# A fused attention, dense MoE and routed MoE kernel: first job's rows loaded earlier, later row loads on GpSimd, scatters declared independent, one low-part subtraction on VectorE

## The chip, the core and the metric

The kernel runs on one core of a Trainium2 chip. That core has five engines with an instruction stream each: PE (TensorE, matrix products), DVE (VectorE), ACT (ScalarE), POOL (GpSimd) and SP (SyncE, here only a queue that issues DMAs). A stream runs in its fixed order; an instruction that waits for another engine or for a transfer holds up all that stand behind it on its own engine. The metric is the time of one execution in microseconds (us); times given are medians of several runs.

## The reference

Three stages follow each other, in float32:

- attention on q, k, v of shape (4, 8, 768, 64), causal with a local window of 96 keys and 8 global keys, a linear bias by distance and a softmax; its output is 3072 tokens of 512 features;
- a dense expert layer: `h = x @ w_in` (512 to 2048), `g = h - tanh(h)`, `x = g @ w_out` (2048 to 512);
- a routed layer with 8 experts: `logits = x @ w_gate`, each token goes to `argmax`; per expert `relu(x @ w1[e]) @ w2[e]` (512 to 1024 to 512), scaled by the softmax value of the chosen expert and a sigmoid of `x @ w_output_gate`.

The result is the 3072 by 512 output of the routed layer.

## The kernel before

**Products in parts.** Each float32 operand of a big product is split into a high part (rounded, made on ACT) and a low part (the difference, made on DVE or POOL); a product is the three matmuls high x high, high x low, low x high. Names end in `h` and `l`: `gh` and `gl` of the gate, `xTh` and `xTl`, `h2h` and `h2l` of an expert's hidden layer, `eh` and `el` of an expert's weights.

**The block phase.** Tokens are worked through in 12 blocks (`NBLK`) of 256. For a block, 16 units of 128 hidden features follow each other: `moe_h` (L607, 12 matmuls into `ph`), the gate on ACT and DVE ending in `gg` (L637), its high part `gh` on ACT (L643) and its low part `gl` (L645, on DVE in the first block and on POOL in the others), then `moe_y` (L662, 6 matmuls into `y`). Attention of later blocks is interleaved.

**Routing of a block.** `rt_evac` copies `y` to `yrow` (ACT L677, DVE L679), `rt_T` transposes it (`yT`, L689), `rt_logits` makes the logits (`lp` L704, `lg` L712), DVE makes the choice, `rk` (L762, L763) counts on PE what place the token has within its expert, and DVE turns that into the row `su` (L787). Two indirect DMAs of POOL (`scatter`, L793) then write the block's 256 rows to those places of `srt`, a DRAM buffer with a region per expert. The framework makes each scatter wait for the one before it, since both write `srt`; only the last two are declared independent.

**The expert phase.** Work is cut into nine jobs. Job 0 is the first 256 rows of the fullest expert, job 1 the rest of that expert, jobs 2 to 8 are the other seven experts. After block 9 the fullest expert must have 256 rows (an assertion in the code says so), so job 0 needs no scatter later than that of block 9. A job is: `ex_rows` loads its rows from `srt` (`xr`, L923, issued by SP), `ex_T` transposes them on PE (`xTp`, L941) and splits them (ACT L954, DVE L955; L960 and L961 copy two columns), `ex_s1` is the first product (`h2p`, L973; `h2h` L977 on ACT, `h2l` L978 on DVE), `ex_s2` the second (`ob`, L1000), `ex_out` scales the result (L1013, L1015) and POOL stores it (L1018). `ex_load` brings an expert's weights in eight 512 KB pieces (`ex`, L881 and L884, issued by SP) into three shared row buffers (tag `row`); `ex_split` makes `eh` (ACT L899) and `el` (DVE L900) of each.

**What sets the order.** For the block phase and jobs 0 and 1 an agenda does: `at(time, rank, function)` puts a function on a slot, and slots are run in order (block `b` starts at 32 b, a unit takes two slots; rank -2 is run with raised priority). Later jobs are written out in a loop. The framework then settles each engine's order from this and from its own estimate of when things are ready, so that a function put earlier can move other engines' instructions too. At L866 `expert(r)` reads the number of the r-th fullest expert into a register of SP, which the DMA addresses need.

**Lines that the change touches.** L644 (who makes `gl`), L793 to L800 (the scatters), L864 to L870 (`expert`), L918 to L923 (`ex_rows`), L1192 to L1196 (job 0's buffers and its slot, `G + 26`, six slots before the end of block 11), L1215 (buffers of the row loads). What lies around them is printed here:

Of the kernel before, what the change touches and what calls it, by code (L numbers as in the profile page):

```python
# [32 lines left out]
def kernel(  # L33
# [15 lines left out]
    nc = tc.nc  # L49
    P = 128  # L50
# [3 lines left out]
    E, _, F = w1.shape  # L54
    TB = 256
    NBLK = NT // TB
# [8 lines left out]
    RS = NT + CAP  # L65
# [10 lines left out]
    persist = ctx.enter_context(tc.tile_pool(name="persist", bufs=1))  # L76
# [3 lines left out]
    srt = dram.tile([E * RS, W], F32, name="srt")  # L80
# [31 lines left out]
    order_i = persist.tile([P, E], I32, name="order_i")  # L112
# [19 lines left out]
    def at(gt, rank, fn):  # L132
        agenda.setdefault((gt, rank), []).append(fn)
# [465 lines left out]
    def moe_h(blk, u, gt):  # L599
        fg, fo = divmod(u, 4)  # L600
        ph = bank("h", 2, f"ph{blk}_{u}")
        n = 0
        for kc in range(KC):
            o = kc * 512 + fo * P
            whi, wlo = wih[fg][:, o : o + P], wil[fg][:, o : o + P]
            for lw, xx in ((whi, xhi), (whi, xlo), (wlo, xhi)):
                nc.tensor.matmul(ph[:, 0:TB], lw, xx[blk][:, kc, :], start=(n == 0), stop=(n == 3 * KC - 1))  # L607
                n += 1

        def tmp(tag, bufs, dt=F32):  # L610
            t = p1.tile([P, TB], dt, tag=tag, bufs=bufs, name=f"{tag}{blk}_{u}")
            return t

        L = {}

        def gate():
            hps = ph[:, 0:TB]
            uu = L["uu"] = tmp("uu", 2)
            ss = L["ss"] = tmp("ss", 2)
            tt = L["tt"] = tmp("tt", 2)  # L620
            vv = L["vv"] = tmp("vt", 2)
            nc.scalar.activation(uu, hps, AF.Square)  # L622
            nc.scalar.activation(tt, hps, AF.Tanh)  # L623
            nc.scalar.activation(ss, uu, AF.Square, scale=G_S, bias=ga[:, 0:1])  # L624
            nc.vector.scalar_tensor_tensor(out=vv, in0=uu, scalar=G_C, in1=hps, op0=ALU.add, op1=ALU.mult)  # L625
            nc.vector.tensor_tensor(out=tt, in0=tt, in1=hps, op=ALU.subtract)  # L626
            nc.vector.scalar_tensor_tensor(out=vv, in0=ss, scalar=G_S2B, in1=vv, op0=ALU.add, op1=ALU.mult)

        def gate2():
            uu, ss, tt, vv = L["uu"], L["ss"], L["tt"], L["vv"]  # L630
            gg = L["gg"] = tmp("gg", 2)
            if blk < 1:
                nc.scalar.activation(ss, uu, AF.Relu, bias=nt2[:, 0:1])
            else:
                nc.vector.tensor_scalar(out=ss, in0=uu, scalar1=G_T2, scalar2=None, op0=ALU.is_gt)
            nc.vector.tensor_tensor(out=gg, in0=vv, in1=uu, op=ALU.mult)
            nc.vector.copy_predicated(gg, ss.bitcast(I32), tt)  # L637

        def parts():
            gg = L["gg"]  # L640
            gh = tmp("gh", 3, F32R)
            gl = tmp("gl", 3, F32R)
            nc.scalar.copy(gh, gg)  # L643
            by = nc.vector if blk < 1 else nc.gpsimd  # L644
            by.tensor_tensor(out=gl, in0=gg, in1=gh.bitcast(F32), op=ALU.subtract)  # L645
            g_t[blk, u] = (gh, gl)

        at(gt + 1, 0, gate)
        at(gt + 2, 0, gate2)
        at(gt + 3, 0, parts)  # L650
# [16 lines left out]


    rts = {}
    last_rows = []  # L670

    def rt_evac(blk):
        for j in range(2):
# [24 lines left out]
    def rt_logits(blk, gt):  # L698
# [92 lines left out]
        def scatter(j):  # L791
            r = rts.pop((blk, "row", j))
            store = nc.gpsimd.indirect_dma_start(  # L793
                out=srt[:, :], out_offset=IndirectOffsetOnAxis(ap=L["su"][:, j : j + 1], axis=0),
                in_=r[:, 0:W], in_offset=None, bounds_check=E * RS - 1, oob_is_err=False,
            )
            if blk == NBLK - 1:
                last_rows.append(store.ins)
                if j == 1:
                    tc.declare_no_dep(last_rows[1], last_rows[0], reason="each token has one row")  # L800

        last = blk == NBLK - 1
        rk = -2 if last else 0
# [31 lines left out]
    ordering = {}  # L835
# [25 lines left out]
        nc.vector.tensor_scalar(out=kk, in0=kk, scalar1=-1.0, scalar2=float(E), op0=ALU.mult, op1=ALU.add)  # L861
        nc.vector.tensor_copy(order_i, kk)

    def expert(r):  # L864

        if r not in ordering:  # L866
            ordering[r] = nc.values_load(
                order_i[0:1, r : r + 1], engines=[mybir.EngineType.SP], min_val=0, max_val=E - 1
            )
        return ordering[r]  # L870


    w1h, w1l, w2h, w2l = {}, {}, {}, {}
# [43 lines left out]

    def ex_rows(n):  # L918
        r, j0, _ = jobs[n]
        rv = expert(r)  # L920
        for j, m in tiles(n):
            t = job_tile(n, "xr", [P, W], F32, f"xr{n}_{j}")
            nc.sync.dma_start(t[0:m, :], srt[ds(rv * RS + (j0 + j) * P, m), :])  # L923
            xrows[n, j] = t

    def tiles(n):
# [248 lines left out]
    for blk in range(NBLK):  # L1175
        G = 32 * blk
# [11 lines left out]
    for i in range(NP):  # L1188
# [2 lines left out]

    pools.update({  # L1192
        ("xTh", 0): (p1, "xhi", 2), ("xTl", 0): (p1, "xlo", 2), ("hh", 0): (p1, "gh", 3), ("hl", 0): (p1, "gl", 3),
        ("orow", 0): (persist, "row", 3),
    })
    at(G + 26, 0, lambda: ex_rows(0))  # L1196
    for g in range(n_groups(0)):
        at(G + 28 + g, 4, lambda g=g: ex_T(0, g))
    G += 32
# [12 lines left out]

    pa.release()
    p2a = ctx.enter_context(tc.tile_pool(name="p2a", bufs=1, side="right", reuse_waits="tile"))
    for k in range(3):  # L1215
        pools["xr", k] = p2a, "xr", 4
    for nm in ("xTh", "xTl"):
        pools[nm, 1] = p2a, "xTa", 4
# [200 lines left out]
```

## Time and profile before

| | |
|---|---|
| median of three runs | 1173.21 us (1171.07 to 1173.40) |
| profiled execution | 1168.82 us |
| its span, first to last instruction | 1167.1 us |
| mean granted TensorE clock | 0.988 |
| PE busy | 1106.7 us (95% of the span) |
| DVE busy | 856.2 us (73%) |
| ACT busy | 671.6 us (58%) |
| POOL busy | 214.2 us (18%) |
| all DMA | 103.25 MB, mean 88 GB/s |

The busy time of an engine is when it executes; PE's 60 us without work are in the first 120 us, around the change from the blocks to the experts (about 800 to 820 us), at a few job changes, and at the end. The profiled execution lies 4.4 us under the median of the runs, and its span 1.7 us under its own time. A granted clock of 1.00 is TensorE at 2.4 GHz and 0.50 is 1.2 GHz; a mean lies between these two levels.

### The profile page before, as it was taken

The page shows a single profiled execution, that of the slowest core. Times are in us where ns is not written, and L with a number is a line of the kernel's source. Part 1 is how long each engine was busy: PE and PEld are TensorE (multiplying, and loading weights), DVE is VectorE, ACT ScalarE, POOL GpSimd, SP SyncE. Part 2 cuts the span into 40 slices and gives each one's busy share as a digit, 9 for nine tenths or more (in the row PEclk, how much of TensorE's full clock was granted, in tenths as well). Part 3 has the DMA queues.
Part 4 walks back from the last instruction along what each step waited for, and adds up shares of the span by engine and source line. Part 5 has one row for each costly group of instructions (what it writes and reads, how often), then busy time and mean ns, then how long its engine had stood idle before and what let it go on. Part 6 is the DMA issues. An engine that isn't in the chain of part 4 may idle for free. (4 is left out here: it accounts for less than half of the span.)

```text
span 1167.1 us, 22211 instructions
## 1 busy us (share of the span) xinstructions
PE 1106.7 (95%) x7374; PEld 943.5 (81%) x7374; DVE 856.2 (73%) x2704; ACT 671.6 (58%) x1794; POOL 214.2 (18%) x281
## 2 busy tenths in 40 slices
PE   2888999999999999999999999998999999999995
PEld 1457888888888888888888888886888787888894
DVE  6899778899989889989889898998554434424411
ACT  4999876666666656666666666565352423423411
POOL 1000013222222222222222232324100100101100
PEclk9889999999999999999999999999999999999998
DMA  6954921111211112121112120113372614526200
GB/s 170 291 165 142 254 58 42 30 51 30 55 38 40 37 39 52 31 55 27 51 24 56 37 53 22 33 67 127 113 246 103 206 53 153 181 61 222 79 23 25
DMA packets 128850, 103.25 MB, mean 88 GB/s; under 512 B 101679, under 2 KB 101679, under 8 KB 128720
## 3 DMA queue, kind: packets, MB, share of 16 engines
q1 hardware_dynamic: 124592, 89.06, 26.7%
q0 software_dynamic: 4128, 12.61, 2.8%
q8 instruction: 62, 1.02, 0.4%
q14 instruction: 68, 0.56, 0.2%
HBM read 90.04 MB, written 21.88 MB: 96 GB/s over the span
## 5 line engine op out<-in xcount | busy, mean ns | idle before, releaser
L645 POOL TENSOR_TENSOR gl<-gg,gh 128x256 fp32r<-128x256 f32 x176 | 149.1, 847 | 485.7 <-ACT gh L643 368.1
L607 PE MATMUL ph<-xhi,wh 128*128 128x256 f32 x768 | 219.9, 289 | 3.5 <-DVE tt L626 3.5
L607 PE MATMUL ph<-xhi,wl 128*128 128x256 f32 x768 | 218.2, 285 | 0.0
L607 PE MATMUL ph<-xlo,wh 128*128 128x256 f32 x768 | 216.2, 282 | 0.0
L662 PE MATMUL y<-wh,gh 128*128 128x512 f32 x384 | 158.2, 412 | 1.0 <-ACT gh L643 0.9
L607 PEld LDWEIGHTS ph<-xhi,wh 128*128 128x128 f32 x768 | 144.8, 189 | 15.9 <-DVE tt L626 5.9
L662 PE MATMUL y<-wl,gh 128*128 128x512 f32 x384 | 154.1, 401 | 0.0
L607 PEld LDWEIGHTS ph<-xlo,wh 128*128 128x128 f32 x768 | 145.0, 189 | 6.7
L607 PEld LDWEIGHTS ph<-xhi,wl 128*128 128x128 f32 x768 | 144.8, 189 | 4.3 <-issue 2.6
L662 PE MATMUL y<-wh,gl 128*128 128x512 f32 x384 | 141.8, 411 | 2.5 <-POOL gl L645 2.3
L643 ACT CAST gh<-gg 128x256 fp32r<-128x256 f32 x192 | 78.2, 407 | 84.9 <-DVE gg L637 66.4
L622 ACT ACTIVATE uu<-ph 128x256 f32<-128x256 f32 x192 | 73.8, 384 | 78.3 <-PE ph L607 70.8
L978 DVE SCALAR_TENSOR_TENSOR h2l<-h2p,h2h 128x448 fp32r<-128x448 f32 (+3 forms) x72 | 40.0, 557 | 103.9 <-ACT h2h L977 103.8
L522 ACT ACTIVATE pr<-pr,sst 128x256 f32<-128x256 f32 (+1 forms) x192 | 93.0, 487 | 38.2 <-DVE sst L514 38.2
L625 DVE SCALAR_TENSOR_TENSOR vt<-uu,ph 128x256 f32<-128x256 f32 x192 | 79.8, 416 | 43.9 <-ACT tt L623 42.6
L900 DVE TENSOR_TENSOR el<-ex,eh 128x1024 fp32r<-128x1024 f32 x64 | 77.7, 1223 | 46.1 <-ACT eh L899 42.2
L977 ACT ACTIVATE h2h<-h2p 128x448 fp32r<-128x448 f32 (+3 forms) x72 | 35.3, 492 | 124.8 <-PE h2p L973 123.9
L899 ACT CAST eh<-ex 128x1024 fp32r<-128x1024 f32 x64 | 66.5, 1050 | 60.2 <-DMA ex<-in_moe_w_dram 45.0
L624 ACT ACTIVATE ss<-uu,ga 128x256 f32<-128x256 f32 x192 | 99.3, 517 | 0.0
L973 PE MATMUL h2p<-xTh,eh 128*128 128x448 f32 (+3 forms) x288 | 97.7, 342 | 0.0
L973 PE MATMUL h2p<-xTl,eh 128*128 128x448 f32 (+3 forms) x288 | 97.2, 338 | 0.0
L973 PE MATMUL h2p<-xTh,el 128*128 128x448 f32 (+3 forms) x288 | 97.1, 338 | 0.0
(199 smaller groups left out, 2505.6 us busy)
## 6 DMA issues: line engine op xcount, KB each, us to landing
ex<-in_moe_w_dram SPq DMA_DIRECT2D x64, 512.0 KB
vv<-vg SPq DMA_DIRECT2D x92, 96.0 KB
srt<-zrow SPq DMA_DIRECT2D x32, 257.0 KB
m<-in_moe_w_in_dram SPq DMA_DIRECT2D x16, 512.0 KB
m<-in_moe_w_out_dram SPq DMA_DIRECT2D x16, 512.0 KB
xr<-srt SPq DMA_DIRECT2D x25, 257.0 KB
qk<-in_q_dram SPq DMA_DIRECT2D x92, 64.0 KB
qk<-in_k_dram SPq DMA_DIRECT2D x92, 64.0 KB
```

Source lines behind the costliest of these rows:

```text
L522: nc.scalar.activation(pr[j][:, c0:], pr[j][:, c0:], AF.Exp, bias=st[:, j : j + 1], scale=-1.0, accum_out=st[:, 2 + j : 3 + j],)
L607: nc.tensor.matmul(ph[:, 0:TB], lw, xx[blk][:, kc, :], start=(n == 0), stop=(n == 3 * KC - 1))
L622: nc.scalar.activation(uu, hps, AF.Square)
L624: nc.scalar.activation(ss, uu, AF.Square, scale=G_S, bias=ga[:, 0:1])
L625: nc.vector.scalar_tensor_tensor(out=vv, in0=uu, scalar=G_C, in1=hps, op0=ALU.add, op1=ALU.mult)
L643: nc.scalar.copy(gh, gg)
L645: by.tensor_tensor(out=gl, in0=gg, in1=gh.bitcast(F32), op=ALU.subtract)
L662: nc.tensor.matmul(yb[blk, j], gx[:, j * P : (j + 1) * P], wx[fg][:, sl], start=(u == 0 and n == 0), stop=(u == NF - 1 and n == 2),)
L899: nc.scalar.copy(hi, st)
L900: nc.vector.tensor_tensor(out=ld[e, t][:, sl], in0=st, in1=hi.bitcast(F32), op=ALU.subtract)
L973: nc.tensor.matmul(ph[:, 0:N], lw, xx, start=(i == 0), stop=(i == 3 * KC - 1))
L978: nc.vector.scalar_tensor_tensor(out=hl, in0=ph[:, 0:N], scalar=0.0, in1=hh.bitcast(F32), op0=ALU.max, op1=ALU.subtract)
```

## The change

Four edits: job 0's rows are loaded at slot `G + 15` rather than `G + 26` (ahead of the scatters of block 10), into other buffers; from job 2 on the rows are loaded by POOL's DMA queue instead of SP's, for which the expert's number is read into a register of POOL too; all scatters to `srt` are declared independent of each other; and `gl` of the last block is made by DVE instead of POOL.

```diff
-            by = nc.vector if blk < 1 else nc.gpsimd
+            by = nc.vector if blk in (0, NBLK - 1) else nc.gpsimd
             by.tensor_tensor(out=gl, in0=gg, in1=gh.bitcast(F32), op=ALU.subtract)
...
-            if blk == NBLK - 1:
-                last_rows.append(store.ins)
-                if j == 1:
-                    tc.declare_no_dep(last_rows[1], last_rows[0], reason="each token has one row")
+
+            tc.declare_no_dep(store.ins, group="srt", reason="each token has one row")
+            tc.add_to_no_dep_group("srt", store.ins)
...
-    def expert(r):
-
-        if r not in ordering:
-            ordering[r] = nc.values_load(
-                order_i[0:1, r : r + 1], engines=[mybir.EngineType.SP], min_val=0, max_val=E - 1
-            )
-        return ordering[r]
+    def expert(r, by=mybir.EngineType.SP):
+
+        if (r, by) not in ordering:
+            ordering[r, by] = nc.values_load(order_i[0:1, r : r + 1], engines=[by], min_val=0, max_val=E - 1)
+        return ordering[r, by]
...
-        rv = expert(r)
+        by, name = (nc.gpsimd, mybir.EngineType.Pool) if n >= 2 else (nc.sync, mybir.EngineType.SP)
+        rv = expert(r, name)
         for j, m in tiles(n):
             t = job_tile(n, "xr", [P, W], F32, f"xr{n}_{j}")
-            nc.sync.dma_start(t[0:m, :], srt[ds(rv * RS + (j0 + j) * P, m), :])
+            by.dma_start(t[0:m, :], srt[ds(rv * RS + (j0 + j) * P, m), :])
...
-        ("orow", 0): (persist, "row", 3),
+        ("orow", 0): (persist, "row", 3), ("xr", 0): (p1, "yt", 3),
     })
-    at(G + 26, 0, lambda: ex_rows(0))
+
+    at(G + 15, 0, lambda: ex_rows(0))
...
-    for k in range(3):
+    for k in range(1, 3):
         pools["xr", k] = p2a, "xr", 4
```

What this does to the order of instructions is shown at three places.

The first is PE, at the end of the block phase, where `y` takes in the last two units of block 11 (`gh_14` to `gl_15`) and job 0 begins (`xTp` are its transposed rows, `h2p` its first product, `ob` its second). Before:

```order
L662 MATMUL y_0_12665<-wh_3_1328,gl_14_13294 128x512 [waits Pool_49]
L662 MATMUL y_1_12666<-wh_3_1328,gl_14_13294 128x512
L662 MATMUL y_0_12665<-wh_3_1328,gh_15_13317 128x512 [waits Activation_49]
...
L941 MATMUL xTp_0_13234<-ident,xr_0_13176 128x128 [waits DMAHW4_49,PE_49]
L941 MATMUL xTp_1_13263<-ident,xr_0_13176 128x128 [waits PE_49]
L662 MATMUL y_0_12665<-wh_3_1328,gl_15_13318 128x512 [waits Pool_49]
L662 MATMUL y_1_12666<-wh_3_1328,gl_15_13318 128x512
L941 MATMUL xTp_0_13234<-ident,xr_1_13178 128x128 [waits DMAHW5_49]
```

Of the changed kernel, the same place; the lines left out at the first dots are twelve matmuls each of `h2p_0` and `h2p_1` and the matmuls of `y` among them:

```order
L970 MATMUL h2p_0_13327<-xTh_0_13239,eh_0_12810 128x256 [waits DVE_49]
...
L970 MATMUL h2p_1_13350<-xTh_0_13239,eh_0_12810 128x256 [waits DVE_49]
...
L662 MATMUL y_0_12665<-wh_3_1328,gl_14_13294 128x512 [waits DVE_49]
L662 MATMUL y_1_12666<-wh_3_1328,gl_14_13294 128x512
L662 MATMUL y_0_12665<-wh_3_1328,gh_15_13317 128x512 [waits Activation_49]
...
L997 MATMUL ob_0_13395<-eh_4_13044,h2h_0_13340 128x512 [waits Activation_49]
...
L662 MATMUL y_0_12665<-wh_3_1328,gl_15_13318 128x512 [waits DVE_49]
L662 MATMUL y_1_12666<-wh_3_1328,gl_15_13318 128x512
L997 MATMUL ob_0_13395<-eh_4_13044,h2l_0_13341 128x512 [waits DVE_49]
```

All of job 0's eight transposes, 24 matmuls of `h2p` and two of `ob` now stand ahead of the last two of `y`; before, two transposes did.

The second is PE from the end of block 11's routing (`rk`, whose `ohb` is the choice of expert) to the first work of job 1 (`xTp` of `xr` after it). Before:

```order
L1000 MATMUL ob_0_13395<-eh_4_13040,h2h_3_13470 128x512 [waits Activation_49]
L763 LDWEIGHTS ones_bf
L763 MATMUL rk_13491<-ohb_13480,ones_bf 128x8 [waits DVE_49]
L1000 MATMUL ob_0_13395<-el_4_13041,h2h_3_13470 128x512
...
L1000 MATMUL ob_0_13395<-eh_6_13131,h2l_6_13588 128x512 [waits DVE_49]
L1000 MATMUL ob_1_13396<-eh_6_13131,h2l_6_13588 128x512
L941 MATMUL xTp_0_13673<-ident,xr_0_13669 128x128 [waits DMAHW2_49,PE_49]
L941 MATMUL xTp_1_13682<-ident,xr_0_13669 128x128
L941 MATMUL xTp_0_13673<-ident,xr_1_13671 128x128 [waits DMAHW3_49]
```

Of the changed kernel; the dots stand for five matmuls of `ob`, the two rows of `cnt_c` (the final counts), and five more of `ob`:

```order
L997 MATMUL ob_0_13395<-eh_6_13135,h2h_6_13587 128x512 [waits Activation_49]
L762 LDWEIGHTS ones_bf
L762 MATMUL rk_13491<-ohb_13480,ones_bf 128x8 [waits DVE_49]
L997 MATMUL ob_0_13395<-el_6_13136,h2h_6_13587 128x512
...
L997 MATMUL ob_1_13396<-eh_6_13135,h2l_7_13611 128x512
L938 MATMUL xTp_0_13673<-ident,xr_0_13669 128x128 [waits DMAHW2_49,PE_49]
L938 MATMUL xTp_1_13682<-ident,xr_0_13669 128x128 [waits DVE_49]
L938 MATMUL xTp_0_13673<-ident,xr_1_13671 128x128 [waits DMAHW3_49]
```

Before, 36 matmuls of `h2p`, 23 of `ob` and the counts stand between the last `rk` and the first `xTp` of job 1; now 11 of `ob` and the counts do, and the routing has moved back behind three more units of job 0.

The third is SP, where the rows of a later job and the weights of its successor are issued (`xr_0` to `xr_3`, `ex_1` to `ex_4`). Before:

```order
L881 DMA ex_2_14046<-in_moe_w_dram 128x1024 [waits DMAHW6_49,DMAHW3_49,DVE_49]
L923 ISA
L923 DMA xr_0_14062<-srt 128x514 [waits DMAHW7_49,PE_49]
L923 ISA
L923 DMA xr_1_14064<-srt 128x514 [waits DMAHW0_49,PE_49]
L923 ISA
L923 DMA xr_2_14066<-srt 128x514 [waits DMAHW1_49,PE_49]
L923 ISA
L923 DMA xr_3_14068<-srt 64x514 [waits PE_49]
L881 ISA
L881 DMA ex_3_14087<-in_moe_w_dram 128x1024 [waits DMAHW4_49,DVE_49]
```

Of the changed kernel:

```order
L877 DMA ex_1_14017<-in_moe_w_dram 128x1024 [waits DMAHW6_49,DVE_49]
L877 ISA
L877 DMA ex_2_14056<-in_moe_w_dram 128x1024 [waits DMAHW7_49,DMAHW2_49,DVE_49]
L877 ISA
L877 DMA ex_3_14107<-in_moe_w_dram 128x1024 [waits DMAHW3_49,DMAHW0_49,DVE_49]
L880 ISA
L880 DMA ex_4_14142<-in_moe_w_dram 128x2x512 [waits DMAHW1_49,DVE_49]
```

The four row loads, which wait for PE, no longer stand between `ex_2` and `ex_3`; they are in POOL's stream, between the stores of finished jobs.

## Rows read from the trace of the kernel before

**Rows 1.** First part of the page: busy time, share of span, instructions.

```profile
PE 1106.7 (95%) x7374; PEld 943.5 (81%) x7374; DVE 856.2 (73%) x2704; ACT 671.6 (58%) x1794; POOL 214.2 (18%) x281
```

**Rows 2.** Waits by releaser, PE and SP: total us, times, longest.

```profile
PE ob L1000 <- ACT h2h L977: 3.5, 2, 1.8
...
PE ob L1000 <- issue: 0.8, 2, 0.4
...
SPq L923 <- PE xTp L941: 114.7, 7, 26.6
```

**Rows 3.** Window at the transition: length, then busy us by engine, clock.

```profile
800.00:820.00 20.00, 15.15 (x87) 11.42 (x86) 15.55 (x33) 10.31 (x21) 9.32 (x9) 1.00 0.40 133
```

**Rows 4.** Timeline of PE, end of blocks: start, us, work, idle before.

```profile
809.41 0.73 PE L662 MATMUL y<-wh,gl 128*128 128x512 f32 x2 [1.67 <-POOL gl L645]
...
814.63 0.41 PE L941 MATMUL xTp<-ident,xr 128*128 128x128 f32 x2 [1.66 <-DMA xr<-srt]
814.79 0.71 PE L662 MATMUL y<-wh,gl 128*128 128x512 f32 x2
...
818.23 0.29 PE L973 MATMUL h2p<-xTh,eh 128*128 128x256 f32 x1
818.35 0.28 PE L973 MATMUL h2p<-xTl,eh 128*128 128x256 f32 x1
```

**Rows 5.** Timelines of PE, DVE, POOL and SP, routing to job 1.

```profile
830.88 0.18 PE L763 MATMUL rk<-ohb,ones_bf 128*128 128x8 bf16 x1
...
832.34 0.17 DVE L787 CAST su<-sf 128x2 uint32<-128x2 f32 x1
...
834.75 0.98 POOL L793 DMA_INDIRECT srt<-yrow,su  x1 [0.30 <-issue]
...
837.91 0.88 SPq L923 DMA_DIRECT2D xr<-srt  x2
...
841.32 0.88 PE L941 MATMUL xTp<-ident,xr 128*128 128x128 f32 x6 [0.16 <-DMA xr<-srt]
...
842.74 0.39 PE L1000 MATMUL ob<-el,h2h 128*128 128x512 f32 x1
842.97 0.63 PE L1000 MATMUL ob<-eh,h2l 128*128 128x512 f32 x2
843.44 0.40 PE L973 MATMUL h2p<-xTh,eh 128*128 128x256 f32 x2
```

**Rows 6.** Lines view: `gl` of the first and last block, `gg` of the last.

```profile
L645 DVE TENSOR_TENSOR gl<-gg,gh 128x256 fp32r<-128x256 f32 x16 | 6.7, 420 | 2.1 <-ACT gh L643 1.9
L645 POOL TENSOR_TENSOR gl<-gg,gh 128x256 fp32r<-128x256 f32 x16 | 16.5, 1033 | 27.1 <-ACT gh L643 26.1 <-POOL gl L645 0.9
L636 DVE TENSOR_TENSOR gg<-vt,uu 128x256 f32<-128x256 f32 x16 | 7.8, 485 | 0.0
```

**Rows 7.** Windows after three waits of PE, clock third from the end.

```profile
50.00:58.00 8.00, 7.40 (x23) 3.17 (x22) 6.42 (x14) 7.87 (x21) 0.00 (x0) 0.57 1.01 351
104.00:110.00 6.00, 4.34 (x22) 3.26 (x23) 4.50 (x15) 6.00 (x19) 0.61 (x3) 0.72 0.44 150
966.00:974.00 8.00, 8.00 (x39) 6.37 (x39) 7.07 (x13) 5.65 (x8) 0.00 (x0) 1.00 0.87 300
```

**Rows 8.** Timelines of PE: the waits ahead of the first two windows.

```profile
49.76 0.66 PE L546 MATMUL pt<-ident,pr 128*128 128x128 f32 x4 [2.23 <-ACT wl L270]
105.46 0.47 PE L546 MATMUL pt<-ident,pr 128*128 128x128 f32 x1 [2.45 <-ACT pr L533]
```

**Rows 9.** Timelines of SP, DVE and ACT at a job change.

```profile
955.97 2.09 SPq L923 DMA_DIRECT2D xr<-srt  x4
958.32 0.37 SPq L881 DMA_DIRECT2D ex<-in_moe_w_dram  x1
...
952.76 1.23 DVE L900 TENSOR_TENSOR el<-ex,eh 128x1024 fp32r<-128x1024 f32 x1 [1.11 <-ACT eh L899]
...
964.36 1.04 ACT L899 CAST eh<-ex 128x1024 fp32r<-128x1024 f32 x1 [3.21 <-DMA ex<-in_moe_w_dram]
```

More of the change, by code (lines that the diff above doesn't have):

```diff
@@ L669 @@
     rts = {}
-    last_rows = []
     def rt_evac(blk):
```

## The prediction, written before the result was known

> **What bounds the kernel now.** Read the share of the engines first: PE is busy 1106.7 us, 95% of the span [rows 1]. The other engines matter only where PE waits for them, so the next view is the list of waits, and then the timeline of PE at the places that the change touches. There are two kinds. The first is the end of block 11. In the 20 us from 800 on PE works 15.15 us [rows 3], so 4.85 us are lost. The timeline shows who ends the longest waits: 1.67 us for a low part from POOL and 1.66 us for job 0's rows, which SP had asked for only just before [rows 4]. Of the 4.85 us some 0.4 come behind the last two matmuls of `y`, which end at 815.5 (814.79 + 0.71, [rows 4]); 4.45 come ahead of them. DVE is full in that block too: no idle time stands ahead of its 16 products into `gg` [rows 6]. The second kind is in the expert phase: two waits of PE for `h2h`, 3.5 us together [rows 2]. All that the change can gain is these 8 us; the rest of PE's idle time is elsewhere.
>
> **The wait ahead of job 1: what the change moves here.** This is the term that decides. Job 1's rows can be loaded only when block 11 has been routed and scattered. The rows give the chain: the last `rk` matmul ends at 831.06, `su` is made at 832.34, the second scatter ends at 835.73 (834.75 + 0.98), SP issues the loads at 837.91 and the transposes of the second 128 rows start at 841.32 [rows 5]: 10.3 us from `rk` to there. Before, 36 matmuls of `h2p` at 0.12 us (818.23 to 818.35, [rows 4]) and 23 of `ob` at 0.23 us (842.74 to 842.97, [rows 5]) stand in this time, 9.7 us of work, and PE waits only 0.16 us. In the changed order the loads of job 0 come early, the framework puts 24 `h2p`, two `ob` and six more transposes ahead of the last `y`, and the routing slides back behind three more units of job 0. Between the last `rk` and job 1's transposes 11 matmuls of `ob` are left: 11 x 0.23 = 2.5 us, with the counts and two transposes about 2.8. PE then waits 10.3 - 2.8 = 7.5 us. Nothing else of job 1 or later can stand in, since PE's order is fixed.
>
> Now the sum from the end of `y` to job 1's first `h2p`. Before, 815.5 to 843.44 is 27.9 us, of which 0.4 idle. Moved ahead of `y`: 24 x 0.12 = 2.9, two `ob` 0.5, six transposes 0.7, in all 4.1. Left are 27.9 - 0.4 - 4.1 = 23.4 us of work. Add the wait of 7.5. Add 0.8, an estimate, because the split of job 1's transposed rows was covered by six matmuls of `ob` (six of 0.23 between the transposes and 843.44, [rows 5]) and is now bare. 31.7 us against 27.9: +3.8.
>
> The end of `y` itself: 4.1 us of work move into 4.45 us of idle time, so it may come 0.35 earlier, not more. What could push it later is the load of the weight piece `ex_7`, which waits for a scatter of block 10 and whose cast stands in ACT's order ahead of gate work; I give this up to 1.5. I take -0.1. The term is +3.7 us. Its bounds: the wait could be 2 us shorter or longer, about what passes between the end of the scatter and SP's issue (835.73 to 837.91, [rows 5]), and with the two ends of `y` that gives +1.5 to +7.
>
> **The clock.** After a wait of 2.23 us early in the kernel [rows 8] the granted clock is 0.57 over the next 8 us [rows 7]: PE at its 1.2 GHz level for most of them, 8 x 0.43 = 3.4 us lost. After one of 2.45 us [rows 8] it is 0.72 over 6 us, 1.7 us lost [rows 7]. Behind the wait of 1.8 us at a job change [rows 2] it stays at 1.00 [rows 7]. A wait of 7.5 us is longer than either that was followed by a fall, so I expect one. It costs between 0 and 3.4; I take 2.5, halfway between the two falls. The Trainium skill, "TensorE: Matmul & The Clock Gate", section "Why this matters for your kernels", asks that PE not idle for some microseconds between bursts of matmuls, since its clock then falls to half; by this rule a loss follows here. The two waits of [rows 8] agree with it.
>
> **The low parts on DVE.** 16 subtractions leave POOL and go to DVE. One takes 420 ns on DVE and 1033 ns on POOL in the mean of the last block [rows 6]. DVE being full, 16 x 0.42 = 6.7 us would come on top. But its own operations seem drawn out while POOL works: the product into `gg`, of the same shape as a low part, takes 485 ns in this block against those 420 [rows 6], and a unit has five operations of this shape on DVE; 16 x 5 x 0.065 = 5.2 us would come back if all were drawn out alike. I take what is added and what is given back as about equal, so nothing on `y`. If DVE gets little back, `y` ends later by up to the 1.5 of the bound above: PE ends 815.5 only after two waits of 1.66 us or more that were not DVE's [rows 4], and these are reserve.
>
> **Scatters independent.** The second scatter of a block no longer waits for the first to land. No wait of PE ends on this except through the low parts queued behind it on POOL in block 11, and these leave POOL anyway. Zero, from -0.2 to 0.2.
>
> **Register reads on POOL.** Seven new ones stand among block 10's low parts. No row shows one on POOL; between these subtractions POOL has idle time (27.1 us around 16 of them, [rows 6]). Zero, at most +1.
>
> **Row loads from job 2 on.** SP loses 25 loads and the waits in front of them, 114.7 us [rows 2]. What stands behind such a load on SP is the next weight piece. At one job change `el` has freed a row buffer at 953.99 (952.76 + 1.23), but SP first issues four row loads, 2.09 us from 955.97 on, and the piece only at 958.32; ACT then waits 3.21 us for it until 964.36 [rows 9], and PE waits for the `h2h` queued behind that cast. Without the loads the piece can go at 954.0, 4.3 us sooner, more than the 3.21. So both waits, 3.5 us, should go. Bounds: 0, if a transfer or a buffer takes the place of the queue, and -4.3 with the two waits of 0.4 that have no releaser [rows 2]. I take -3.5.
>
> For POOL the loads are new. They stand ahead of stores of finished rows, and job 2's stand behind job 0's two stores, so they are issued while PE waits for job 1's rows. A DMA that POOL prepares took it about 1 us (0.98 with 0.30 between, [rows 5]): two stores and four loads are 8 us from the end of job 0's last `ob`; job 2's transposes come 7.5 + 1 + 1.7 = 10.2 us after it, or later at the lower clock. The last rows, 3.4 us in landing (837.91 to 841.32, [rows 5]), may be 1 to 2 us late. I take 0, because the lower clock stretches the matmuls in front, and keep 0 to +2. The Trainium skill, "DMA: Bandwidth & Descriptors", section "Latency and other measured facts", gives a GpSimd DMA about 1 us to its first byte against 0.6; no run shown here has such a load from GpSimd. By that the sum would be 0.4 higher if it fell on PE's path.
>
> **Sum.** +3.7 + 2.5 + 0 - 3.5 = +2.7 us on the profiled execution's 1168.82 is 1171.5. This execution lies 4.4 us under the median of the timed runs, so the forecast in the terms of that median is 1175.9 us.
>
> **Rivals.** All are worked out against the median.
> - *Faster.* The wait ahead of job 1 is at its short end (+1.5), does not pull the clock down, and the expert phase gains all 4.3 us: 1173.2 + 1.5 - 4.3 = 1170.4. For it: both small waits stand at the same `ob` as the two large ones [rows 2]. Against it: the wait would have to keep the clock up at three times the length after which it fell twice. It decides from the point where wait and clock together cost under 2 us.
> - *No change.* The wait is there and the clock does not fall: 3.7 - 3.5 = +0.2, 1173.4. For it: at the transition PE has worked without a break for 20 us or more before the wait, and in the first 120 us it had not.
> - *Slower by more.* SP's queue was not what held up the weights, or POOL's stores now do: the change does not do what it says in the expert phase, and the two waits stay. 3.7 + 2.5 + 0 = +6.2: 1179.4. For it: from its issue at 958.32 to the cast at 964.36 the piece needed 6 us, more than the queue had cost it [rows 9]. Against it: the row buffer was free 4.3 us before the issue.
>
> **How the numbers follow.** What a measurement of this kernel can tell from no change is about 0.2%, 2.3 us: faster is below 1170.9, slower above 1175.5. The forecast has 0.50, between 1174 and 1178.5; of this 0.33 lies above 1175.5 and 0.17 below. Faster has 0.21, no change 0.18 (0.01 of it below 1170.9), slower by more 0.11. Sums: faster 0.22, same 0.34, slower 0.44. The range from 1169.5 to 1179.5 takes in the forecast, no change, about half of the faster case and half of the slowest. The forecast alone has 1174 to 1178.5.
>
> **What would show it.** Right: PE waits 5 to 9 us for `xr` ahead of job 1's transposes, and no more than 0.5 us at a time ahead of the last `y`; the granted clock is near 0.5 for some microseconds behind that wait; there is no wait of PE for `h2h` over 1 us at later job changes, and ACT's waits for `ex` are shorter. Wrong: a wait ahead of job 1 under 4 us; a granted clock of 1.00 all through; waits for `h2h` still there; waits of PE for `xr` in jobs 2 to 8; or DVE so late in block 11 that `y` ends over 1.5 us later, counted from the start of the block.

## The result, and the profile after

The changed kernel takes 1183.01 us (median of four runs, 1181.03 to 1184.86), the kernel before 1172.14 us beside it (1170.42 to 1173.40). The ratio is 1.0093 with a 95% interval of 1.0071 to 1.0116: about 11 us slower. The forecast was 1175.9 us, from 1169.5 to 1179.5. The sign was right; the size was wrong, above the range. The profiled execution took 1183.32 us, its span is 1181.6 us and its mean granted clock 0.977 (0.988 before).

The list of waits of PE in the changed kernel (us in total, times, longest) shows the exchange that the change made:

```profile
PE xTp L938 <- DMA xr<-srt: 7.6, 2, 6.7
PE y L662 <- ACT gh L643: 5.9, 4, 3.5
...
PE h2p L970 <- ACT xTh L951: 1.5, 1, 1.5
PE ob L997 <- ACT h2h L974: 1.5, 3, 0.8
```

The wait for `h2h` at the job changes, 3.5 us in [rows 2], is down to 1.5, as hoped. The waits for POOL's low parts and for job 0's rows in [rows 4] are gone. In their place stand 7.6 us for job 1's rows, 5.9 us for `gh` in the block phase and 1.5 us for `xTh`.

The windows around the transition (length, busy us of PE, PEld, DVE, ACT and POOL, granted clock, DMA share, GB/s) show where the time is lost; [rows 3] is the first of them before:

```profile
800.00:820.00 20.00, 15.36 (x89) 13.29 (x88) 16.70 (x47) 9.79 (x22) 3.12 (x4) 0.91 0.39 132
820.00:840.00 20.00, 20.00 (x136) 17.58 (x135) 8.89 (x27) 7.60 (x15) 0.00 (x0) 1.00 0.17 54
840.00:860.00 20.00, 10.83 (x55) 8.32 (x54) 5.45 (x23) 3.92 (x7) 6.23 (x8) 0.74 0.60 205
860.00:880.00 20.00, 19.57 (x120) 17.77 (x119) 12.06 (x26) 8.82 (x16) 2.16 (x4) 0.91 0.58 183
```

From 840 to 860 PE works 10.83 of 20 us, and a part of that at the 1.2 GHz level (mean clock 0.74). Two more falls of the clock show as 0.91 in the first and the last window.

The two profiled executions are 2.5 us apart already where block 0's `yT` begins (161.4 and 163.9 in the two timelines), ahead of the first scatter, and no further where block 9's `yT` begins (722.2 and 724.8). The lost clock accounts for it (7.8 and 10.3 us of busy time times missing clock up to 162 us; from 24 to 36 us the clock is 1.00 in the kernel before and 0.53 in the changed one), and the experiments below begin block 0's `yT` at 160.5 to 164.3 us whatever was edited. So this table, read from PE's timelines, counts in each kernel the us from block 9's `yT`:

| us from block 9's `yT` to | before | changed | difference |
|---|---|---|---|
| end of the last `y` of block 11 | 93.3 | 98.2 | +4.9 |
| end of the last `rk` | 108.8 | 117.2 | +8.4 |
| job 1's first `h2p` | 121.2 | 129.8 | +8.6 |
| end of the last `ob` | 432.1 | 443.0 | +10.9 |

The 10.9 us of the last row agree with the 10.9 between the medians. They fall into three parts: 4.9 ahead of the end of `y`, 3.7 from there to job 1's first `h2p`, and 2.3 behind it, in which the gain of the expert phase is already taken off.

**The end of `y`.** In the timelines of ACT and PE of the changed kernel at the end of block 11 (start, us, work, idle before and what ended it) one cast holds up the gates:

```profile
811.46 1.04 ACT L895 CAST eh<-ex 128x1024 fp32r<-128x1024 f32 x1 [2.92 <-DMA ex<-in_moe_w_dram]
812.41 0.38 ACT L623 ACTIVATE tt<-ph 128x256 f32<-128x256 f32 x1
...
813.34 0.40 ACT L643 CAST gh<-gg 128x256 fp32r<-128x256 f32 x1
...
813.80 0.79 PE L662 MATMUL y<-wh,gh 128*128 128x512 f32 x1 [3.54 <-ACT gh L643]
...
822.32 0.63 PE L662 MATMUL y<-wh,gl 128*128 128x512 f32 x2
```

The cast at 811.46 is that of the weight piece `ex_7`. It waits 2.92 us for its transfer. Behind it on ACT stand the last step of unit 13's gate (its `gh`, at 813.34) and the gates of units 14 and 15, and so PE waits 3.54 us. The piece itself is late because SP could not issue it: its row buffer is one of the three that also hold block 10's `yrow`, and SP waits for the scatter of those rows to land. In the waits of SP from 780 to 815 us this is one row:

```profile
SPq L880 <- DMA srt<-yrow,su: 5.2, 1, 5.2
```

In the kernel before, the same cast stood behind the gate of unit 14, and the same late transfer cost PE only 0.23 us (timelines of ACT and PE before):

```profile
807.89 0.40 ACT L643 CAST gh<-gg 128x256 fp32r<-128x256 f32 x1 [0.45 <-DVE gg L637]
810.37 1.05 ACT L899 CAST eh<-ex 128x1024 fp32r<-128x1024 f32 x1 [2.07 <-DMA ex<-in_moe_w_dram]
811.32 0.40 ACT L643 CAST gh<-gg 128x256 fp32r<-128x256 f32 x1
...
811.77 0.50 PE L662 MATMUL y<-wh,gh 128*128 128x512 f32 x1 [0.23 <-ACT gh L643]
```

The clock falls behind the wait of 3.54 us: in windows of 2 us (columns as above) it is

```profile
812.00:814.00 2.00, 0.20 (x1) 0.20 (x2) 1.47 (x2) 2.00 (x6) 0.10 (x1) 0.87 0.36 147
814.00:816.00 2.00, 2.00 (x6) 1.62 (x7) 2.00 (x7) 1.49 (x3) 0.11 (x1) 0.50 0.00 0
```

**From routing to job 1.** The rows that answer to [rows 5], timelines of PE, DVE, POOL, SP and ACT:

```profile
841.78 0.18 PE L762 MATMUL rk<-ohb,ones_bf 128*128 128x8 bf16 x1
...
842.97 0.17 DVE L786 CAST su<-sf 128x2 uint32<-128x2 f32 x1
...
845.32 0.97 POOL L792 DMA_INDIRECT srt<-yrow,su  x1 [0.30 <-issue]
...
848.41 0.87 SPq L920 DMA_DIRECT2D xr<-srt  x2
...
851.48 0.66 PE L938 MATMUL xTp<-ident,xr 128*128 128x128 f32 x2 [6.73 <-DMA xr<-srt]
853.01 1.54 PE L938 MATMUL xTp<-ident,xr 128*128 128x128 f32 x6 [0.87 <-DMA xr<-srt]
...
857.77 1.04 ACT L895 CAST eh<-ex 128x1024 fp32r<-128x1024 f32 x1 [3.23 <-DMA ex<-in_moe_w_dram]
858.72 0.58 ACT L951 CAST xTh<-xTp 128x512 fp32r<-128x512 f32 x1
...
859.35 0.51 PE L970 MATMUL h2p<-xTh,eh 128*128 128x256 f32 x2 [1.53 <-ACT xTh L951]
```

The chain from `rk` to job 1's transposes has the length it had (11 us, 10.3 before), and PE now waits through it, 6.73 + 0.87 us. Then the second half of job 1's `xTh` stands on ACT behind the cast of another late weight piece, which costs PE 1.53 us more. The clock is at 0.50 behind the long wait:

```profile
850.00:852.00 2.00, 0.52 (x2) 0.29 (x2) 0.21 (x2) 0.00 (x0) 0.49 (x1) 0.50 0.96 309
854.00:856.00 2.00, 1.97 (x8) 1.34 (x7) 0.69 (x1) 0.54 (x1) 1.08 (x2) 0.50 1.00 363
```

The matmuls of `h2p` behind the wait follow each other every 0.21 us, where before it was 0.12 [rows 4]:

```profile
855.70 0.42 PE L970 MATMUL h2p<-xTh,el 128*128 128x256 f32 x1
855.91 0.42 PE L970 MATMUL h2p<-xTh,eh 128*128 128x256 f32 x1
```

Not all of this time is lost. The cast behind which `xTh` stands began at 857.77, when its transfer let it, so a faster PE would have waited there longer than 1.53 us.

Busy time times missing clock, summed over the windows of 2 us from 780 to 900, is 5.8 us (none before): 1.46 behind the wait for `gh`, 2.65 behind the wait for job 1's rows and 1.64 behind the wait for `xTh`. The idle time of PE in the same stretch is 14.7 us (5.2 before).

**DVE.** With the low parts on DVE four of its six other operations of a unit are shorter. Lines of the last block, first two of the changed kernel, which answer to [rows 6], then one operation before and after the change:

```profile
L636 DVE TENSOR_TENSOR gg<-vt,uu 128x256 f32<-128x256 f32 x16 | 6.8, 424 | 0.0
L645 DVE TENSOR_TENSOR gl<-gg,gh 128x256 fp32r<-128x256 f32 x16 | 6.7, 423 | 0.1
...
L635 DVE TENSOR_SCALAR ss<-uu 128x256 f32<-128x256 f32 x16 | 7.0, 441 | 0.3
...
L635 DVE TENSOR_SCALAR ss<-uu 128x256 f32<-128x256 f32 x16 | 4.7, 294 | 0.1
```

The product into `gg` takes 424 ns instead of 485, the comparison into `ss` 294 instead of 441. The two operations that read `ph` (L625, L626) took 412 and 410 ns before and take 418 now.

### The profile page after: what moved, and what is told of

It is laid out like the page before. It is cut to its first block, busy times and chain, and to the rows that moved or that the text cites. A ratio compares the mean times of both kernels' runs of the same rounds, so it can differ in the third digit from the quotient of the medians.

```text
span 1181.6 us, 22254 instructions
## 1 busy us (share of the span) xinstructions
PE 1110.5 (94%) x7374; PEld 949.0 (80%) x7374; DVE 851.4 (72%) x2720; ACT 670.6 (57%) x1794; POOL 217.1 (18%) x290
## 4 chain that ended last, share of the span: by engine, by line
PE 78%; ACT 6%; DVE 5%; DMA 5%; issue 3%; SPq 1%; POOL 0%; POOLq 0%; DVEq 0%; ACTq 0%
PE y L662 21%; PE ph L607 20%; PE ob L997 11%; PE h2p L970 11%; PE xp L560 4%; PE sc L497 4%; PE pt L546 3%; DMA ex<-in_moe_w_dram 2%; DVE el L896 1%; PE pk L433 1%; PE yT L688 1%; DMA vv<-in_v_dram 1%; PE xTp L938 1%; ACT eh L895 1%; PE pq L430 1%
## 5 line engine op out<-in xcount | busy, mean ns | idle before, releaser
L645 POOL TENSOR_TENSOR gl<-gg,gh 128x256 fp32r<-128x256 f32 x160 | 131.7, 823 | 487.0 <-ACT gh L643 362.6
L625 DVE SCALAR_TENSOR_TENSOR vt<-uu,ph 128x256 f32<-128x256 f32 x192 | 80.0, 417 | 44.4 <-ACT tt L623 43.5
L997 PE MATMUL ob<-eh,h2h 128*128 128x512 f32 x232 | 92.9, 400 | 1.5 <-ACT h2h L974 1.5
```

The source lines that it names most:

```text
L997: nc.tensor.matmul(ob[n, j][0:m, :], gx[:, j * P : j * P + m], wx, start=(f == 0 and i == 0), stop=(f == NF2 - 1 and i == 2),)
```

## The experiments

All medians are of kernels timed beside the kernel before, whose own median was 1170.3 to 1171.1 us in these series; what counts is the ratio to it. The theory to be tested: PE's order has put block 11's routing behind job 0's work, so job 1's rows come late (A), and a cast that waits for a late weight piece stands ahead of the last gates (G). The rivals put the loss on one of the four edits by itself.

### One edit at a time

**Row loads from job 2 on by GpSimd** (`pool_rows_only`): the edits of `expert` and `ex_rows` alone.

> Only the row loads from job 2 on go to GpSimd; everything else as before. PE's order up to job 1 is that of before (36 h2p and 23 ob between rk and job 1's transposes). Theory A (the loss is the routing that slid back behind job 0's work, so job 1's rows are late): the transition is as before (wait ahead of job 1 under 0.5 us), the two waits for h2h at job changes are gone, about 3.5 us faster than before, 1168 to 1170. Rival B (GpSimd's row loads, with their stores and register reads, cost more than they give): PE waits for xr in jobs 2 to 8, and the kernel is not faster than before, 1172 or more.

Measured: 1166.97 us, ratio 0.9969 (0.9951 to 0.9987), 3.6 us faster. PE's waits in this kernel:

```profile
PE ob L999 <- ACT h2h L976: 1.7, 3, 0.7
PE xTp L940 <- DMA xr<-srt: 1.6, 1, 1.6
```

The waits for `h2h` fall from 3.5 us with a longest of 1.8 [rows 2] to 1.7 with a longest of 0.7; the one wait for `xr` is the old one for job 0. B falls: this part of the change pays, and in this order it costs nothing elsewhere that shows.

**Low parts of the last block on DVE** (`low_dve_only`):

```diff
-            by = nc.vector if blk < 1 else nc.gpsimd
+            by = nc.vector if blk in (0, NBLK - 1) else nc.gpsimd
```

> Only the low parts of the last block go to DVE. By itself this makes the framework put 24 h2p, two ob and all transposes of job 0 ahead of the last y, and leaves 11 ob between rk and job 1's transposes. Theory A: PE waits 7 to 8 us ahead of job 1, the clock falls behind that wait, the waits for h2h at later job changes stay: 8 to 14 us slower than before, 1180 to 1186. Rival C (it is the early load of job 0's rows that costs): within 2 us of before.

Measured: 1183.44 us, ratio 1.0089 (1.0055 to 1.0122). One changed engine name costs as much as the whole change. PE's timeline in this kernel:

```profile
811.33 0.50 PE L662 MATMUL y<-wh,gh 128*128 128x512 f32 x1 [4.87 <-ACT gh L643]
...
851.99 0.66 PE L941 MATMUL xTp<-ident,xr 128*128 128x128 f32 x2 [6.30 <-DMA xr<-srt]
```

Both waits of the changed kernel are there, though job 0's rows are loaded where they were before. C falls.

**Job 0's rows earlier** (`early_rows_only`): `G + 26` to `G + 15`, and the buffers.

> Only job 0's rows are loaded earlier. PE's order again: 5 h2p and 12 ob (3.4 us) between rk and job 1's transposes. Theory A: a wait of 6.5 to 7.5 us ahead of job 1 with a fall of the clock behind it, 5 to 12 us slower than before, 1177 to 1184, with the waits for h2h at later job changes still there. Rival D (it is the low parts on DVE that cost): within 2 us of before or faster, since the wait of 1.66 us for job 0's rows is gone.

Measured: 1178.27 us, ratio 1.0046 (1.0017 to 1.0075).

```profile
817.81 0.50 PE L662 MATMUL y<-wh,gh 128*128 128x512 f32 x1 [1.92 <-ACT gh L643]
...
846.88 0.66 PE L941 MATMUL xTp<-ident,xr 128*128 128x128 f32 x2 [5.28 <-DMA xr<-srt]
```

The same two waits, shorter. D falls too: either edit is enough.

**Scatters independent** (`scatters_only`): the edit at L793 to L800 alone.

> Only the scatters are declared independent. PE's order: 22 h2p and 18 ob (6.9 us) between rk and job 1's transposes, 2 h2p ahead of the last y. Theory A (routing behind job 0's work makes job 1's rows late): a wait of 3 to 4 us ahead of job 1, a fall of the clock possible, the waits for h2h at later job changes as before: 2 to 6 us slower than before, 1173 to 1177. Rival F (the scatters in themselves are free and order does not matter at this size): within 1 us of before.

Measured: 1178.66 us, ratio 1.0074 (1.0057 to 1.0091), 8.7 us slower, where A gave it 6 at most.

```profile
842.87 2.16 PE L939 MATMUL xTp<-ident,xr 128*128 128x128 f32 x8 [2.98 <-DMA xr<-srt]
...
840.00:860.00 20.00, 17.09 (x94) 15.16 (x95) 9.73 (x24) 7.59 (x13) 1.95 (x2) 0.83 0.79 262
```

The wait of 2.98 us is about as long as A says, and it brings the clock down to 0.83 over 20 us. F falls: an edit that takes a wait away and adds no work makes the kernel slower by the order that follows from it. The profiled execution is the fastest of the four, at 1175.07 us, 4.6 above the median of the kernel before, so its trace can't hold all of the 8.7 us. In it some 1.4 us are a second fall, behind a later wait for `h2h` of 2.16 us (0.66 over 1062 to 1066, so 4 × 0.34); the rest of what A lacks stays open.

### The order put right

**Routing first** (`all_routing_first`): the whole change, and job 0's units 5 to 7 queued on PE behind block 11's last `rk`. `issue_after` sets an order on one engine and adds no wait.

```diff
+    def ex_s1_after(f):
+        with tc.issue_after(last_rk[0].ins):
+            ex_s1(0, f)
...
-            at(G + 1 + 2 * f, 4, lambda f=f: ex_s1(0, f))
+            at(G + 1 + 2 * f, 4, lambda f=f: ex_s1_after(f) if f >= 5 else ex_s1(0, f))
```

> The whole change, and PE's matmuls of job 0's units 5 to 7 (h2p) are queued behind block 11's last rk matmul, which puts rk back behind unit 4 and 36 h2p and 18 ob between it and job 1's transposes (8.5 us of work for the chain of 10.3). Theory A: the wait ahead of job 1 falls from 7.6 to under 2.5 us, the clock stays at 1.00 behind it, and 7 to 11 us come back: 1172 to 1176. Rival E (what costs is the late end of y and the full DVE): only the waits for job 1's rows move elsewhere, 1180 or more.

Measured: 1170.33 us, ratio 0.9994 (0.9978 to 1.0010).

```profile
812.37 0.78 PE L662 MATMUL y<-wh,gh 128*128 128x512 f32 x1 [3.38 <-ACT gh L643]
...
845.62 0.41 PE L941 MATMUL xTp<-ident,xr 128*128 128x128 f32 x2 [1.91 <-DMA xr<-srt]
847.17 1.75 PE L941 MATMUL xTp<-ident,xr 128*128 128x128 f32 x7 [1.13 <-DMA xr<-srt]
```

The wait ahead of job 1 falls from 7.6 to 3.0 us (2.5 were expected at most) and 11.6 us of the median come back, 1.0093 to 0.9994 of 1170, more than the 7 to 11 expected. The waits of 1.53 and 0.43 us at job 1's start are gone as well. The clock still falls behind these 3 us, which A had not expected. E falls. The wait for `gh` stays, as it must.

**Gates first** (`all_gates_first`): the whole change, and the splits of `ex_7` and of the next expert's first piece queued on ACT and DVE behind the last `gh` and `gl`.

```diff
+    def ex_split_after(e, i):
+        with tc.issue_after(last_gate[0].ins), tc.issue_after(last_gate[1].ins):
+            ex_split(e, i)
...
-        at(G + 12 + 2 * i, 0, lambda i=i: ex_split(0, i))
+        if i < 7:
+            at(G + 12 + 2 * i, 0, lambda i=i: ex_split(0, i))
+        else:
+            at(G + 34, 4, lambda i=i: ex_split_after(0, i))
...
-        at(G + 5 + 2 * steps[i], 4, lambda i=i: ex_split(1, i))
+        at(G + 5 + 2 * steps[i], 4, lambda i=i: ex_split(1, i) if i else ex_split_after(1, i))
```

> The whole change, and on ACT and DVE the split of the weight piece ex_7 and of the next expert's first piece is queued behind the last gate of block 11. PE's routing order is nearly that of the change (6 h2p and 12 ob between rk and job 1's transposes). Theory G (y ends late because the cast of ex_7 waits for a load that waits for a scatter, ahead of gate work): the wait of 3.5 us for gh is gone, y ends 3.5 to 5 us earlier, the wait ahead of job 1 stays at 6 to 7.5 us, 1176 to 1179. Rival H (y ends late because DVE is full): another wait of PE takes its place, y ends as late as in the changed kernel, 1181 to 1184.

Measured: 1170.97 us, ratio 1.0012 (0.9999 to 1.0026); better than expected. The wait of 3.5 us is gone, `y` ends 92.7 us after block 9's `yT` (93.3 before, 98.2 in the changed kernel), and what is left is this:

```profile
841.43 0.66 PE L943 MATMUL xTp<-ident,xr 128*128 128x128 f32 x2 [5.05 <-DMA xr<-srt]
842.66 1.54 PE L943 MATMUL xTp<-ident,xr 128*128 128x128 f32 x6 [0.57 <-DMA xr<-srt]
```

H falls: with the low parts on DVE and the cast out of the way `y` ends no later than before. The expectation was short because it did not count the first fall of the clock, nor the waits of 1.53 and 0.43 us at job 1's start, which are gone here too, nor that this kernel's last `rk` stands nearer to the end of `y` (18.3 us behind it, 19.0 in the changed kernel).

**Both** (`all_both_first`).

> The whole change with both: the split of ex_7 behind the last gate, and job 0's units 5 to 7 behind block 11's last rk. Theories A and G together: y ends 3.5 to 5 us earlier than in all_routing_first, the wait ahead of job 1 stays at 2 to 3 us, and the kernel beats that one by 3.5 to 6 us: 1164 to 1167, faster than before and than pool_rows_only. Rival H: no more than 1 us better than all_routing_first, 1169 to 1171.

Measured: 1166.13 us, ratio 0.9967 (0.9953 to 0.9980). A and G together make a kernel that is slower than before into one that is faster, with all four edits kept. The two gains do not add up (11.6 and 9.5 us alone, 14.8 together), since either order by itself also takes away the waits at job 1's start and a part of the lost clock.

**Both, low parts on GpSimd** (`both_first_low_on_pool`).

> As all_both_first, but the low parts of the last block stay on GpSimd. If GpSimd's low parts hold y up by themselves, as the two waits of 0.6 and 1.7 us in the kernel before say: 1.5 to 3 us slower than all_both_first. If their cost is only that they slow DVE down, and DVE has room now: the same within 1 us.

Measured: 1167.19 us, ratio 0.9975 (0.9956 to 0.9993): no difference from the last that these intervals can tell. Once the order holds, it does not show here who makes the low parts.

### The clock

**The wait filled** (`all_filled_wait`): the whole change with matmuls that nothing uses in the wait.

```diff
-                nc.tensor.matmul(
+                last_ob[n] = nc.tensor.matmul(
...
     ex_rows(1)
+    fill = bank_a("fill")
+    with tc.issue_after(last_ob[0].ins):
+        for i in range(28):
+            nc.tensor.matmul(fill, w1h[0, 0][:, 0:P], w1h[0, 0][:, 512:1024], start=True, stop=True)
```

> The whole change, with 28 matmuls of 128x512 (6 us at 2.4 GHz) on weights already loaded, into a bank that nothing reads, between job 0's last ob and job 1's transposes: PE works through most of its wait of 7.6 us. They add no useful work. Theory K (the fall of the clock behind that wait costs as much as the product of busy time and missing clock says, 4.3 us in the changed kernel): the clock stays at 1.00 from 845 to 870 and the kernel is 3 to 6 us faster than the changed one, 1177 to 1180. Rival L (the clock's fall is hidden, since PE waits there anyway for weights and rows): within 1.5 us of the changed kernel, 1182 to 1184.

Measured: 1177.24 us, ratio 1.0054 (1.0034 to 1.0074), 4.6 us less than the changed kernel's 1.0093. But the clock did not stay up:

```profile
853.17 1.04 PE L939 MATMUL xTp<-ident,xr 128*128 128x128 f32 x6 [2.40 <-DMA xr<-srt]
...
852.00:858.00 6.00, 4.65 (x24) 4.04 (x25) 2.85 (x7) 2.85 (x4) 1.08 (x2) 0.72 1.03 387
```

The matmuls ended 2.4 us too early, and the clock fell behind that. The fall is shorter: busy time times missing clock is 3.0 us from 780 to 900, 2.7 less. The added instructions also put both halves of `xTh` ahead of the late cast, which takes away 1.5 us of waiting and a further 0.4 beside it. 2.7 + 1.9 is 4.6, the difference measured; the split between the two is worked out from the windows and not tested by itself, and in this trace PE's waits after 880 us are 1.4 us longer (3.0 against 1.5), so the agreement is in part chance. The kernel comes out where K said, but not by K's way: the clock fell, and the order on ACT moved too. L's range (1182 to 1184) is missed; since 1.9 of the 4.6 us belong to the moved order, and the intervals are 2 us to either side, this run does not settle L. In the changed kernel the wait for `xTh` does hide a part of the fall, as L says. In `all_routing_first` nothing can: there `h2p` goes at 0.21 us behind the fall, and PE waits for nothing from 847 to 971 us.

### Towards a better version

**Job 2's rows by SP** (`both_first_low_pool_job3`): as both_first_low_on_pool, with `n >= 3` in place of `n >= 2` in `ex_rows`.

> As both_first_low_on_pool, but GpSimd loads the rows only from job 3 on, and SP those of job 2. If job 2's rows come late because GpSimd issues them behind job 0's stores (waits of 1.4 and 0.8 us for xr around job 1's start): 1 to 2.5 us faster than both_first_low_on_pool, 1164 to 1166. If SP's four loads hold up the weights there, as they did at job changes: 0 to 3 us slower, 1167 to 1170.

Measured: 1161.73 us, ratio 0.9925 (0.9904 to 0.9945), 8.8 us faster than the kernel before, 2 us better than expected and the best of all.

```profile
838.50 0.41 PE L946 MATMUL xTp<-ident,xr 128*128 128x128 f32 x2 [0.27 <-DMA xr<-srt]
839.11 0.87 PE L946 MATMUL xTp<-ident,xr 128*128 128x128 f32 x6 [0.19 <-DMA xr<-srt]
...
840.00:860.00 20.00, 19.45 (x129) 17.66 (x130) 12.96 (x25) 10.55 (x18) 0.97 (x1) 1.00 0.79 265
```

The waits for rows around job 1's start are 0.5 us in all, and the clock stays at 1.00. In `all_both_first` the row that remained was job 2's:

```profile
842.12 0.47 PE L946 MATMUL xTp<-ident,xr 128*128 128x128 f32 x1 [1.63 <-DMA xr<-srt]
```

**The same with the low parts on DVE** (`all_both_first_job3`).

> As all_both_first, but GpSimd loads the rows only from job 3 on, and SP those of job 2. Job 2's rows late behind GpSimd's stores (waits of 0.9 and 1.6 us for xr): 1 to 2.5 us faster than all_both_first, 1163.5 to 1165.5. SP's loads hold up weights instead: 0 to 3 us slower.

Measured: 1163.27 us, ratio 0.9940 (0.9920 to 0.9961), a little better than expected. It is 1.5 us slower than its twin with the low parts on GpSimd: its six runs (1162.99 to 1165.92) lie above five of the twin's six (1160.55 to 1162.12, the sixth 1163.57). In the pair before, GpSimd's low parts were 1.1 us slower, so no run shows a cause for the 1.5 us.

**Without the scatter edit** (`both_first_no_scatter_edit`): as both_first_low_on_pool with the scatters as before.

> As both_first_low_on_pool, but only the last two scatters are independent, as before. If independent scatters are worth something once the order holds (block 10's buffers come free one landing, about 3 us, sooner, for ex_7): 1 to 3 us slower than both_first_low_on_pool. If not: the same within 1 us.

Measured: 1167.05 us, ratio 0.9961 (0.9941 to 0.9981), as both_first_low_on_pool: independent scatters are worth nothing here that could be measured, as the second branch of the expectation had it.

## Why the prediction was right and wrong, point by point

- **The wait ahead of job 1: right.** Forecast 7.5 us, measured 6.73 + 0.87. From the end of `y` to job 1's first `h2p` the forecast was 31.7 us, the timeline shows 31.6. That this total fits so closely is luck: 1.1 us of it are the half clock, which the forecast had in another term, and the work took 22.9 us where 24.2 were reckoned. `all_routing_first` shows that this order is a cause.
- **What moves the order: wrong.** The prediction put it down to job 0's early rows. The single edits show that the low parts on DVE do it as fully, and the scatters in part. Those two terms were priced at zero by what their instructions take, and each alone makes the kernel slower: 1.0089 and 1.0074.
- **The end of `y`: the step that failed.** The prediction took -0.1 us, with +1.5 as the end of the range, and measured was +4.9. It named the place (the cast of `ex_7` ahead of gate work, behind a scatter) and gave it too little: the stall alone is 3.54 us, and the clock falls behind it, 1.5 us. So the 4.1 us of work that moved ahead of `y` did not fill the 4.45 us of idle time: PE is idle for 5.1 us there again (1.10 and 3.54 for `gh`, two of about 0.2). `all_gates_first` shows that the place of the splits in ACT's and DVE's order is the cause and that the fuller DVE is not.
- **The clock: right in kind, too small.** Forecast 2.5 us with 3.4 as the upper bound, for one fall. That fall, behind the wait for job 1's rows, measured 2.6, of which the wait for `xTh` hides a part. But there were three, 5.8 us by busy time times missing clock. The first, behind the wait for `gh`, was not in the sum; the last follows the 1.53 us for `xTh`. The rule of the Trainium skill that was weighed there ("TensorE: Matmul & The Clock Gate", section "Why this matters for your kernels") has the clock fall behind idle gaps of some microseconds. The runs agree that it falls behind gaps, but not on their length: the waits of 2.23 and 2.45 us in [rows 8], and others of 1.71 to 2.40 us listed at the end of this document, are shorter than the gap that the section names, and the clock fell behind them; behind some of the same length it did not. There the measurement decides.
- **The cast ahead of `xTh`: not seen.** 1.53 us of wait and 0.43 beside it. The prediction had looked at ACT's order ahead of `y` and not behind job 1's transposes. Its 0.8 us for the bare split is the nearest term that it has.
- **The expert phase: right.** Forecast -3.5. The single edit gives 3.6 us in the median. In the changed kernel PE's waits after 880 us fall from 4.3 to 1.5 us in the timelines, 2.7 less.
- **Low parts on DVE, as work: right in the sum, not in its parts.** Of the 6.8 us that are added 4.1 come back, where 5.2 were reckoned; not all operations were drawn out alike, `ss` gives back 147 ns a unit, `gg` 61, and those that read `ph` nothing. With the cast out of the way `y` is not later for it. GpSimd's register reads cost nothing that shows.
- **Job 2's rows: forecast 0, within 0 to 2.** In the changed kernel the longer wait hides them. Where that wait is gone they show: moving them back to SP gave 5.9 us (0.9975 to 0.9925), more than the 2.2 us of waits for `xr`, since the fall of the clock went with them.

The sum with the measured terms: 4.9 for the end of `y`, 3.7 to job 1's first `h2p`, 2.3 behind it (3.2 for the lost clock and 2.0 for the waits at job 1's start, less 2.7 in the expert phase, which leaves 0.2 over), 10.9 us. The forecast had -0.1, 3.8 and -1.0.

What stays open: why in `all_gates_first` PE's waits for `h2h` at job changes are 4.1 us again, five of 0.2 to 1.1, although the rows are loaded by GpSimd there; how far the clock and the order of ACT each carry the gain of the filled wait; and what the early load of job 0's rows is worth once the order holds, since no run has the two pinned orders without it.

## What to carry to other kernels

Where a scheduler settles the order, price an edit by the order it makes and not by its own instructions: look on each engine at what a late transfer's first user stands in front of. In this kernel many waits of PE of about two microseconds and more were paid twice, once as idle time and once as half clock behind it, so the last small waits at a stage change are worth more than they look. When a good edit makes a kernel slower, pin the order at the place of the new wait before giving the edit up: all four edits together were 0.9% slower, and with two pinned orders and job 2's rows left on SP three of them are 0.75% faster.

## What was not expected of the hardware

The length of a wait alone did not tell whether the granted clock would fall. It fell behind waits of 2.23 and 2.45 us [rows 8], of 2.40 us in `all_filled_wait`, 2.16 us in `scatters_only` (0.66 over 1062 to 1066) and 2.02 us in `low_dve_only`. Another of 2.06 us in `low_dve_only` left it at 1.00, as did one of 1.92 us in `early_rows_only` and those of up to 1.8 us at the job changes [rows 2]. Early in the kernel both sides reach further. PE's timelines of the changed kernel and of the kernel before:

```profile
105.83 0.33 PE L546 MATMUL pt<-ident,pr 128*128 128x128 f32 x1 [1.71 <-ACT pr L533]
...
29.56 2.08 PE L268 MATMUL wlo<-m,ident 128*128 128x512 f32 x2 [5.43 <-DVE m L257]
```

Behind the 1.71 us the clock went to 0.50, at about 107 us; with the wait of 5.43 us it was 1.00 from 24 to 36 us. Several waits close together, 0.32, 0.85 and 1.63 us within 5 us in `all_both_first`, brought it down as well (0.83 over 840 to 860), while 0.27 and 0.19 in the best version did not.

GpSimd at work did not draw out DVE's operations alike: of the same 128x256 shape, the product into `gg` took 485 ns with it and 424 without, the comparison into `ss` 441 and 294, and those that read `ph` 410 to 418 either way. In the pair with both orders pinned `ss` took about 415 and 293.
